# Attention and feed-forward fused: from 128-token tiles with tokens on partitions to 512-token chunks with features on partitions

## The chip, the cores and the metric

The program runs on one core of one Trainium2 chip. A core has a matrix engine (PE; its weight loads are listed as PEld), a vector engine (DVE), an activation engine (ACT), a general engine (POOL) and a queue engine (SP), and 16 DMA engines. Each engine works through its own list of instructions in order; semaphores make one wait for another. SBUF is the on-chip memory, 128 partitions wide; PSUM is the small memory that PE writes, 8 banks of 2 KB a partition. The metric is device time in microseconds (us) of one execution, lower is better.

## The reference

Inputs are `q`, `k`, `v` of shape (8, 8, 576, 64): batch B, heads H, sequence S, head width D. There is no softmax over the sequence; each head has a 64x64 matrix `kv`. Everything is float32 outside the kernel.

```python
kv  = einsum('bhsd,bhse->bhde', k, v)
out = einsum('bhsd,bhde->bhse', q, kv)
x   = out / sqrt(mean(out*out, -1) + 1e-6) * g_norm     # per head; then tokens x (H*D = 512)
h   = x @ w_in                                          # 4608 x 1024
sm  = exp(h - max(h)) / (sum(exp(h - max(h))) + 1e-9)
solu = h * sm
ln  = (solu - mean(solu)) / sqrt(var(solu) + 1e-6) * g_ln
return ln @ w_out                                       # 4608 x 512
```

A layer norm takes out any factor that is common to a row, so both kernels leave the division by the softmax sum undone: they normalise `h * exp(h)` instead. The old kernel puts 1e-30 in place of the 1e-6 under the roots.

## The kernel before, in words

Tokens stand on partitions. The batch is taken in four pairs. For each of the two batches of a pair, `phase_A` loads `k` and `v` in tiles of 128 tokens (the fifth tile has 64), multiplies them per head into `kv_ps` and copies each to `kv_sb`; `phase_B` loads a tile of `q`, transposes it head by head on PE (`qtps`, copied to `qtsb`), multiplies by `kv_sb` into `op`, squares on ACT (`osq`), sums per head on DVE (`ssq`), takes Ln and Exp on ACT (`lssq`, `rstd`) for the reciprocal root, scales (`xb`) and transposes back (`xtps`) into `xT`. Then `phase_C` runs for each 128-token tile: 8 matmuls into `hps` (2 PSUM banks), Exp on ACT (`e_sb`), product on DVE (`solu`), statistics on DVE (`stats`, `mv`), Ln and Exp on ACT (`lvar`, `rstd_ln`), normalisation on DVE (`ln`), 8 transposes (`lnTps`), a copy (`lnT`), 8 matmuls (`ops`), a copy on ACT (`obuf`), and the store from SP's queue.

A scheduler orders each engine's instructions by its own estimates, and so mixes the phases of neighbouring tiles. `hps` has one buffer, `lnTps` and `ops` share one, `op`, `qtps` and `xtps` have one each. All loads go through POOL's DMA queue and change float32 to bf16 on the way; each row that a load moves is one head of one token: 64 values, 256 bytes in DRAM. Weights are loaded first, then scaled by `g_norm` and `g_ln` on DVE.

ACT_TABLE_LOAD is an instruction that the compiler puts into ACT's list where the next function is not in the table that is loaded: here between Ln and Exp.

Of the kernel before, what the change touches and what calls it, by code (L numbers as in the profile page):

```python
# [21 lines left out]
):  # L23
    nc = tc.nc
    fp32 = mybir.dt.float32
    bf16 = mybir.dt.bfloat16
# [25 lines left out]
    kv_sb = big.tile([128, B * H, D], bf16)

    g_rep = big.tile([128, 1], fp32)
    nc.gpsimd.dma_start(g_rep[:64, :], g_norm[:, None])
    nc.gpsimd.dma_start(g_rep[64:128, :], g_norm[:, None])
    g_ln_sb = big.tile([128, 8], fp32)
    for nt in range(8):  # L60
        nc.gpsimd.dma_start(g_ln_sb[:, nt:nt + 1], moe_g_ln[nt * 128:(nt + 1) * 128, None])

    with tc.tile_pool(name="wtmp", bufs=2) as wtmp_pool:
        for dt in range(4):
            wt = wtmp_pool.tile([128, d_ff], bf16, name="wt")
            nc.gpsimd.dma_start(wt[:, :], moe_w_in[dt * 128:(dt + 1) * 128, :])
            nc.vector.tensor_scalar_mul(out=w_in_sb[:, dt, :], in0=wt[:, :], scalar1=g_rep[:, :])
        for ntl in range(8):
            wt = wtmp_pool.tile([128, d_model], bf16, name="wt2")
            nc.gpsimd.dma_start(wt[:, :], moe_w_out[ntl * 128:(ntl + 1) * 128, :])  # L70
            nc.vector.tensor_scalar_mul(out=w_out_sb[:, ntl, :], in0=wt[:, :], scalar1=g_ln_sb[:, ntl:ntl + 1])

    kvl = ctx.enter_context(tc.tile_pool(name="kvl", bufs=12))
    kvp = ctx.enter_context(tc.tile_pool(name="kvp", bufs=2, space=bass.MemoryType.PSUM))
    qload = ctx.enter_context(tc.tile_pool(name="qload", bufs=2))
    qt_p = ctx.enter_context(tc.tile_pool(name="qtp", bufs=1, space=bass.MemoryType.PSUM))
    ap_p = ctx.enter_context(tc.tile_pool(name="attp", bufs=1, space=bass.MemoryType.PSUM))
    xtp = ctx.enter_context(tc.tile_pool(name="xtp", bufs=1, space=bass.MemoryType.PSUM))
    qt_s = ctx.enter_context(tc.tile_pool(name="qts", bufs=2))
    rmsp = ctx.enter_context(tc.tile_pool(name="rmsp", bufs=2))  # L80
    moep = ctx.enter_context(tc.tile_pool(name="moep", bufs=1, space=bass.MemoryType.PSUM))
    Cpsum = ctx.enter_context(tc.tile_pool(name="Cpsum", bufs=1, space=bass.MemoryType.PSUM))
    mpool = ctx.enter_context(tc.tile_pool(name="mpool", bufs=2))
    smallp = ctx.enter_context(tc.tile_pool(name="smallp", bufs=3))

    def phase_A(b):
        kstiles = []
        vstiles = []
        for s0, sz in S_TILES:
            ks = kvl.tile([128, H, D], bf16, name="ks")  # L90
            vs = kvl.tile([128, H, D], bf16, name="vs")
            nc.gpsimd.dma_start(ks[:sz, :, :], k[b, :, s0:s0 + sz, :].rearrange("h s d -> s h d"))  # L92
            nc.gpsimd.dma_start(vs[:sz, :, :], v[b, :, s0:s0 + sz, :].rearrange("h s d -> s h d"))
            kstiles.append(ks)
            vstiles.append(vs)
        nst = len(S_TILES)
        for h in range(H):
            kv_ps = kvp.tile([128, D], fp32, name="kv_ps")
            for sti, (s0, sz) in enumerate(S_TILES):
                nc.tensor.matmul(  # L100
                    kv_ps[:D, :], kstiles[sti][:sz, h, :], vstiles[sti][:sz, h, :],
                    start=(sti == 0), stop=(sti == nst - 1),
                )
            nc.scalar.copy(out=kv_sb[:D, b * H + h, :], in_=kv_ps[:D, :])  # L104

    def phase_B(b):
        for s0, sz in S_TILES:
            qtl = qload.tile([128, H, D], bf16, name="qtl")
            nc.gpsimd.dma_start(qtl[:sz, :, :], q[b, :, s0:s0 + sz, :].rearrange("h s d -> s h d"))  # L109
            qtps = qt_p.tile([128, H, 128], bf16, name="qtps")  # L110
            for h in range(H):
                nc.tensor.transpose(qtps[:D, h, :sz], qtl[:sz, h, :], ident[:sz, :sz])  # L112
            qts = qt_s.tile([128, H, 128], bf16, name="qtsb")
            nc.vector.tensor_copy(qts[:D, :, :sz], qtps[:D, :, :sz])  # L114
            op = ap_p.tile([128, H * D], fp32, name="op")
            for h in range(H):
                nc.tensor.matmul(  # L117
                    op[:sz, h * D:(h + 1) * D], qts[:D, h, :sz], kv_sb[:D, b * H + h, :],
                    start=True, stop=True,
                )  # L120
            opr = op.rearrange("p (h d) -> p h d", h=H)
            osq = rmsp.tile([128, H * D], fp32, name="osq")
            nc.scalar.activation(out=osq[:sz, :], in_=op[:sz, :], func=AF.Square)  # L123
            ssq = rmsp.tile([128, H], fp32, name="ssq")
            nc.vector.tensor_reduce(out=ssq[:sz, :], in_=osq.rearrange("p (h d) -> p h d", h=H)[:sz, :, :], axis=AX, op=ADD)
            lssq = rmsp.tile([128, H], fp32, name="lssq")
            nc.scalar.activation(out=lssq[:sz, :], in_=ssq[:sz, :], func=AF.Ln, scale=1.0 / D, bias=eps_t[:sz, :])  # L127
            rstd = rmsp.tile([128, H], fp32, name="rstd")
            nc.scalar.activation(out=rstd[:sz, :], in_=lssq[:sz, :], func=AF.Exp, scale=-0.5, bias=0.0)  # L129
            xb = rmsp.tile([128, H * D], bf16, name="xb")  # L130
            nc.vector.tensor_tensor(  # L131
                out=xb.rearrange("p (h d) -> p h d", h=H)[:sz, :, :],
                in0=opr[:sz, :, :],
                in1=rstd[:sz, :, None].to_broadcast([sz, H, D]),
                op=MUL,
            )
            xbr = xb.rearrange("p (dt c) -> p dt c", dt=4)
            xtps = xtp.tile([128, 4, 128], bf16, name="xtps")
            for dt in range(4):
                nc.tensor.transpose(xtps[:, dt, :sz], xbr[:sz, dt, :], ident[:sz, :sz])  # L140
            tk0 = b * S + s0
            nc.scalar.copy(out=xT[:, :, tk0:tk0 + sz], in_=xtps[:, :, :sz])  # L142

    def phase_C(m):
        t0 = m * 128
        hps = moep.tile([128, d_ff], fp32, name="hps", tag="hps")
        for dt in range(4):
            for nh in range(2):
                nc.tensor.matmul(  # L149
                    hps[:, nh * 512:(nh + 1) * 512],  # L150
                    xT[:, dt, t0:t0 + 128],
                    w_in_sb[:, dt, nh * 512:(nh + 1) * 512],
                    start=(dt == 0), stop=(dt == 3),
                )
        e_sb = mpool.tile([128, d_ff], fp32, name="e_sb")
        nc.scalar.activation(out=e_sb[:, :], in_=hps[:, :], func=AF.Exp)  # L156
        solu = mpool.tile([128, d_ff], fp32, name="solu")
        nc.vector.tensor_tensor(out=solu[:, :], in0=hps[:, :], in1=e_sb[:, :], op=MUL)  # L158
        stats = smallp.tile([128, 2, 6], fp32, name="stats")
        for sg in range(2):  # L160
            nc.vector.bn_stats(out=stats[:, sg, :], in_=solu[:, sg * 512:(sg + 1) * 512])  # L161
        mv = smallp.tile([128, 2], fp32, name="mv")
        nc.vector.bn_aggr(out=mv[:, :], in_=stats[:, :, :])
        lvar = smallp.tile([128, 1], fp32, name="lvar")
# [7 lines left out]
        for ntl in range(8):  # L172
            nc.tensor.transpose(lnTps[:, ntl, :], lnr[:, ntl, :], ident[:, :])  # L173
# [3 lines left out]
        for ntl in range(8):  # L177
            nc.tensor.matmul(ops[:, :], lnT[:, ntl, :], w_out_sb[:, ntl, :], start=(ntl == 0), stop=(ntl == 7))  # L178
# [44 lines left out]
```

## Time and profile before

| | |
|---|---|
| median of 3 runs | 426.84 us (426.75 to 428.88) |
| span of the profiled execution | 427.0 us |
| PE busy | 282.0 us, 66% |
| ACT busy | 301.2 us, 71% |
| DVE busy | 219.5 us, 51% |
| POOL busy | 114.1 us, 27% |
| mean granted clock of PE | 0.844 |

No total of its own is listed for the profiled execution beside its span. The span lies 0.2 us above the median and inside the range of the runs, so what lies around it is taken as nothing, and sums are made against 427.0 us. Busy shares are means over the whole span. A group's "mean ns" is the duration of one instruction; matmuls overlap, so a group of n can be busy for less than n times the mean.

### The profile page before, as it was taken

The numbers are of one execution on the slowest core, as the hardware profiler recorded it, in microseconds if no ns is written. First come the engines' busy times: TensorE is split into PE (matmuls) and PEld (weight loads), VectorE is DVE, ScalarE is ACT, GpSimd is POOL, SyncE is SP. The second block draws the span as 40 slices with busy tenths as digits, with TensorE's granted clock in tenths as the row PEclk, the third lists the DMA queues.
The fourth block names the chain that finished last, engine by engine and source line by source line (L and its number), as shares of the span: only waits on it lengthen the run. The fifth ranks groups of instructions, "written<-read, shape, count | busy, mean of one in ns | idle before, by whom it ended". The sixth has DMA issues, their size and how long they took to land.

```text
span 427.0 us, 5212 instructions
## 1 busy us (share of the span) xinstructions
PE 282.0 (66%) x1984; PEld 147.8 (35%) x1984; DVE 219.5 (51%) x349; ACT 301.2 (71%) x495; POOL 114.1 (27%) x148
## 2 busy tenths in 40 slices
PE   0112775966977874978786828477876966756755
PEld 0112442543533342544343414233332433332222
DVE  0310324654767473556675736447674655456461
ACT  1000567699786777899868787979769689797771
POOL 8459546546280013650000110100010110000000
PEclk9999976688799896868999988667998668569888
DMA  2989979999695254995232441420340331001011
GB/s 37 148 80 138 109 50 92 77 109 124 61 128 77 38 74 28 108 80 54 40 58 57 50 51 13 42 38 11 52 68 25 65 24 32 25 0 51 25 49 49
DMA packets 119768, 26.03 MB, mean 61 GB/s; under 512 B 113600, under 2 KB 114624, under 8 KB 119744
## 3 DMA queue, kind: packets, MB, share of 16 engines
q0 software_dynamic: 114560, 16.27, 55.4%
q1 hardware_dynamic: 5184, 9.44, 6.0%
q8 instruction: 15, 0.25, 0.2%
q14 instruction: 9, 0.07, 0.1%
HBM read 32.51 MB, written 9.44 MB: 98 GB/s over the span
## 4 chain that ended last, share of the span: by engine, by line
ACT 50%; PE 27%; issue 7%; DVE 7%; DMA 5%; POOL 4%; POOLq 0%
ACT L127 9%; PE hps L149 9%; ACT L165 8%; ACT L129 7%; PE ops L178 6%; ACT e_sb L156 6%; ACT L167 5%; PE lnTps L173 3%; PE kv_ps L100 3%; PE xtps L140 3%; DVE ln L169 3%; ACT obuf L180 2%; DVE xb L131 2%; ACT lssq L127 2%; ACT osq L123 2%
## 5 line engine op out<-in xcount | busy, mean ns | idle before, releaser
L149 PE MATMUL hps<-w_in_sb,xT 128*128 128x512 bf16 x288 | 94.6, 446 | 5.7 <-DVE solu L158 5.6
L109 POOL DMA_DIRECT2D qtl<-in_q_dram x40 | 33.7, 842 | 212.7 <-PE qtps L112 159.1
L178 PE MATMUL ops<-w_out_sb,lnT 128*128 128x512 bf16 x288 | 85.0, 441 | 3.5 <-DVE lnT L175 3.4
L131 DVE TENSOR_TENSOR xb<-op,rstd 128x512 bf16<-128x512 f32 (+1 forms) x40 | 27.4, 685 | 77.7 <-ACT rstd L129 77.7
L156 ACT ACTIVATE e_sb<-hps 128x1024 f32<-128x1024 f32 x36 | 36.7, 1020 | 29.4 <-PE hps L149 29.3
L100 PE MATMUL kv_ps<-vs,ks 128*64 128x64 bf16 (+1 forms) x320 | 33.8, 222 | 33.9 <-ACT kv_sb L104 17.8
L169 DVE TENSOR_SCALAR ln<-solu,mv,rstd_ln 128x1024 bf16<-128x1024 f32 x36 | 29.7, 824 | 49.3 <-ACT rstd_ln L167 49.3
L173 PE MATMUL lnTps<-ident,ln 128*128 128x128 bf16 x288 | 27.6, 252 | 39.8 <-DVE ln L169 31.7
L158 DVE TENSOR_TENSOR solu<-hps,e_sb 128x1024 f32<-128x1024 f32 x36 | 43.6, 1212 | 17.4 <-ACT e_sb L156 17.4
L127 ACT ACT_TABLE_LOAD x37 | 47.5, 1283 | 0.7
L161 DVE BATCH_NORM_STATS2 stats<-solu 128x6 f32<-128x512 f32 x72 | 47.0, 676 | 0.0
L104 ACT CAST kv_sb<-kv_ps 64x64 bf16<-64x64 f32 x64 | 11.5, 200 | 49.1 <-PE kv_ps L100 49.1
L112 PE MATMUL qtps<-ident,qtl 128*64 128x128 bf16 (+1 forms) x320 | 31.2, 247 | 21.8 <-DMA qtl<-in_q_dram 19.9
L178 PEld LDWEIGHTS <-lnT 128*128 128x128 bf16 x288 | 28.3, 109 | 42.4 <-issue 16.3
L129 ACT ACT_TABLE_LOAD x33 | 42.3, 1283 | 0.6
L100 PEld LDWEIGHTS <-ks 128*64 128x64 bf16 (+1 forms) x320 | 24.6, 124 | 49.5 <-issue 40.5
L140 PE MATMUL xtps<-ident,xb 128*128 128x128 bf16 (+1 forms) x160 | 17.5, 241 | 36.5 <-DVE xb L131 33.3
L92 POOL DMA_DIRECT2D ks<-in_k_dram x40 | 35.7, 892 | 18.3 <-PE kv_ps L100 14.7
L149 PEld LDWEIGHTS <-xT 128*128 128x128 bf16 x288 | 27.5, 107 | 35.0 <-issue 18.5
L173 PEld LDWEIGHTS <-ln 128*128 128x128 bf16 x288 | 21.5, 114 | 51.3 <-DVE ln L169 47.5
L114 DVE COPY qtsb<-qtps 64x1024 bf16<-64x1024 bf16 (+1 forms) x40 | 24.7, 617 | 27.4 <-PE op L117 25.3
L142 ACT COPY xT<-xtps 128x512 bf16<-128x512 bf16 (+1 forms) x40 | 21.5, 539 | 21.5 <-PE xtps L140 21.2
(32 smaller groups left out, 337.2 us busy)
## 6 DMA issues: line engine op xcount, KB each, us to landing
out_dram<-obuf SPq DMA_DIRECT2D x36, 256.0 KB, 2.0
qtl<-in_q_dram POOLq DMA_DIRECT2D x32, 128.0 KB, 3.4
ks<-in_k_dram POOLq DMA_DIRECT2D x32, 128.0 KB, 4.4
vs<-in_v_dram POOLq DMA_DIRECT2D x32, 128.0 KB, 4.6
wt<-in_moe_w_in_dram POOLq DMA_DIRECT2D x4, 256.0 KB, 5.1
wt<-in_moe_w_out_dram POOLq DMA_DIRECT2D x8, 128.0 KB, 4.1
qtl<-in_q_dram POOLq DMA_DIRECT2D x8, 64.0 KB, 2.6
ks<-in_k_dram POOLq DMA_DIRECT2D x8, 64.0 KB, 4.3
```

The lines of the kernel that those rows point to most:

```text
L92: nc.gpsimd.dma_start(ks[:sz, :, :], k[b, :, s0:s0 + sz, :].rearrange("h s d -> s h d"))
L100: nc.tensor.matmul(kv_ps[:D, :], kstiles[sti][:sz, h, :], vstiles[sti][:sz, h, :], start=(sti == 0), stop=(sti == nst - 1),)
L127: nc.scalar.activation(out=lssq[:sz, :], in_=ssq[:sz, :], func=AF.Ln, scale=1.0 / D, bias=eps_t[:sz, :])
L129: nc.scalar.activation(out=rstd[:sz, :], in_=lssq[:sz, :], func=AF.Exp, scale=-0.5, bias=0.0)
L131: nc.vector.tensor_tensor(out=xb.rearrange("p (h d) -> p h d", h=H)[:sz, :, :], in0=opr[:sz, :, :], in1=rstd[:sz, :, None].to_broadcast([s ...
L149: nc.tensor.matmul(hps[:, nh * 512:(nh + 1) * 512], xT[:, dt, t0:t0 + 128], w_in_sb[:, dt, nh * 512:(nh + 1) * 512], start=(dt == 0), stop ...
L156: nc.scalar.activation(out=e_sb[:, :], in_=hps[:, :], func=AF.Exp)
L158: nc.vector.tensor_tensor(out=solu[:, :], in0=hps[:, :], in1=e_sb[:, :], op=MUL)
L161: nc.vector.bn_stats(out=stats[:, sg, :], in_=solu[:, sg * 512:(sg + 1) * 512])
L169: nc.vector.tensor_scalar(out=ln[:, :], in0=solu[:, :], scalar1=mv[:, 0:1], scalar2=rstd[:, :], op0=SUB, op1=MUL)
L173: nc.tensor.transpose(lnTps[:, ntl, :], lnr[:, ntl, :], ident[:, :])
L178: nc.tensor.matmul(ops[:, :], lnT[:, ntl, :], w_out_sb[:, ntl, :], start=(ntl == 0), stop=(ntl == 7))
```

## The change

The whole body is rewritten, and the order of work on each engine is now the order in which it is written (`manual_schedule`).

- **Layout.** A chunk has 512 tokens. Chunks 0 to 7 are the first 512 tokens of the 8 batches; chunk 8 is the 64 left-over tokens of all 8. Features stand on partitions and tokens on the free axis, for `q` (transposed on PE into `qT_ps`), `x_sb` and `h_ps`. `u_sb` (the product `h * exp(h)`) is then the stationary operand of the last matmul as it is, so `xtps`, `lnTps` and their copies are gone.
- **Loads.** `load_main` brings 512 tokens of a batch in one DMA, four neighbouring tokens of a head to a row: 1,024 bytes in DRAM. `load_rem` brings the 64 left-over tokens. Loads of a batch are issued three chunks ahead. The weights come in float32 over SP's queue.
- **Attention.** `kvbd` holds two heads' matrices on a block diagonal, so one 128x512 matmul makes `o_ps` for two heads. The sum of squares over a head is a matmul with `head_mean` (`s_ps`); Ln, Exp (`lss`, `rst`) and the scaling then work on 128x512 tiles, 4 for each chunk.
- **Statistics.** POOL squares `u` (`usq_sb`) and adds pairs of `e` (`es_sb`). Twenty matmuls with 32-column weights (`stat_sel`, four groups of columns in turn) sum squares, `u` and `e` over the features into `sum_ps`; DVE copies it to `sums`; four float32 matmuls bring it to tokens on partitions (`st_ps`); DVE and ACT make `rstd` from it.
- **Layer norm folded.** `w_out_sb` is `g_ln * w_out` less its mean over the features (`mean_ps`), which takes out the mean of `u`; `rstd` is applied when the result leaves PSUM (`out_evac`, on DVE).
- **Tables.** One table that has Exp, Ln and Square is loaded at the start.
- **Pipeline.** Chunk c has 8 slots. In slot s PE makes `h_ps` of c, a part of the attention of c+1 (in slot 6 the `kv` of c+2), and half of one output tile of c-1.

```diff
+    ctx.enter_context(tc.manual_schedule())
+    epool = ctx.enter_context(tc.tile_pool(name="epool", bufs=4))
+    ph = ctx.enter_context(tc.tile_pool(name="ph", bufs=2, space=PSUM))
+    po = ctx.enter_context(tc.tile_pool(name="po", bufs=2, space=PSUM))
+    pst = ctx.enter_context(tc.tile_pool(name="pst", bufs=1, space=PSUM))
+    pat = ctx.enter_context(tc.tile_pool(name="pat", bufs=3, space=PSUM))
+    nc.scalar.preload_act_table_set("natural_log_exp_and_others")
...
+    def s_mm(c, p):
+        t = pat.tile([128, 512], FP32, name="s_ps", tag="at")
+        nc.tensor.matmul(t[:, :], head_mean[:, :], osq_sb.pop(p)[:, :], start=True, stop=True)
+        lss = work.tile([128, 512], FP32, name="lss")
+        nc.scalar.activation(out=lss[:, :], in_=t[:, :], func=AF.Ln, bias=eps_t[:, :])
+        rst = work.tile([128, 512], FP32, name="rst")
+        nc.scalar.activation(out=rst[:, :], in_=lss[:, :], func=AF.Exp, scale=-0.5, bias=zero_t[:, :])
+        nc.vector.tensor_tensor(out=x_sb[c][:, p, :], in0=o_ps.pop(p)[:, :], in1=rst[:, :], op=MUL)
...
+    def h_step(c, f):
...
+        t = ph.tile([128, 512], FP32, name="h_ps")
+        for dt in range(NP):
+            nc.tensor.matmul(
+                t[:, :], w_in_sb[:, dt, f * 128:(f + 1) * 128], x_sb[c][:, dt, :],
+                start=(dt == 0), stop=(dt == NP - 1),
+            )
...
+        nc.scalar.activation(out=e[:, f % 2, :], in_=t[:, :], func=AF.Exp, bias=zero_t[:, :])
+        nc.vector.tensor_tensor(out=u_sb[c][:, f, :], in0=t[:, :], in1=e[:, f % 2, :], op=MUL)
+        nc.gpsimd.tensor_tensor(out=usq_sb[c][:, f, :], in0=u_sb[c][:, f, :], in1=u_sb[c][:, f, :], op=MUL)
+        if f % 2 == 1:
+            nc.gpsimd.tensor_tensor(out=es_sb[c][:, f // 2, :], in0=e[:, 0, :], in1=e[:, 1, :], op=ADD)
...
+    def stats(c):
+        t = pst.tile([128, 512], FP32, name="sum_ps", tag="st")
...
+        for n, (i, mov) in enumerate(todo):
+            j = n % 4
+            nc.tensor.matmul(
+                t[32 * j:32 * j + 32, :], stat_sel[:, i, :], mov,
+                start=(n < 4), stop=(n >= len(todo) - 4), tile_position=(0, 32 * j),
+            )
+        sums = work.tile([128, 512], FP32, name="sums")
+        nc.vector.tensor_copy(sums[:, :], t[:, :])
+        st_ps = pst.tile([128, 4, 3], FP32, name="st_ps", tag="st")
+        for m in range(4):
+            nc.tensor.matmul(st_ps[:, m, :], sums[:, m * 128:(m + 1) * 128], stat_pick[:, :], start=True, stop=True)
...
+    for c in range(NC + 1):
+        for s in range(8):
+            if c < NC:
+                h_step(c, s)
+            if c >= 1 and s == 0:
+                stats(c - 1)
+            if c == 0:
+                if s < 4:
+                    for f in (2 * s, 2 * s + 1):
+                        nc.gpsimd.tensor_scalar_mul(
+                            out=w_out_g[:, f, :], in0=w_out_f[:, f, :], scalar1=g_ln_sb[:, f:f + 1]
+                        )
+                if s == 5:
...
+                        nc.tensor.matmul(mean_ps[:, :], col_mean[:, :], w_out_g[:, f, :], start=(f == 0), stop=(f == NF - 1))
...
+            if c + 1 < NC:
+                a = c + 1
...
+                if s == 0:
+                    qT(a, 0)
+                if s == 1:
+                    qT(a, 1)
+                    o_mm(a, 0)
+                if 2 <= s <= 5:
+                    s_mm(a, s - 2)
+                    if s < 5:
+                        o_mm(a, s - 1)
+                if s == 6 and c + 2 < B:
+                    kv_mm(c + 2)
+                    kv_evac(c + 2)
+            if s == 2 and c + 3 < B:
+                load_main(ks, kvl, k, c + 3, "ks")
...
+            if c >= 1:
+                out_half(c - 1, s // 2, s % 2)
+                if s % 2 == 1:
+                    out_evac(c - 1, s // 2)
```

**ACT, in the middle of the program.** Before, from one Ln of the attention (`lssq`) to the next:

```order
L127 ACT_TABLE_LOAD
L127 ACTIVATE lssq<-ssq,eps_t 128x8
L129 ACT_TABLE_LOAD
L129 ACTIVATE rstd<-lssq 128x8
L165 ACT_TABLE_LOAD
L165 ACTIVATE lvar<-mv,eps_t 128x1
L167 ACT_TABLE_LOAD
L167 ACTIVATE rstd_ln<-lvar 128x1
L156 ACTIVATE e_sb<-hps 128x1024
L142 COPY xT<-xtps 128x4x128
L123 ACTIVATE osq<-op 128x512
```

The same engine now, in slots 1 to 3 of a chunk (line numbers are those of the changed kernel):

```order
L206 ACTIVATE osq<-o_ps,zero_t 128x512
L234 ACTIVATE e_sb<-h_ps,zero_t 128x512
L212 ACTIVATE lss<-s_ps,eps_t 128x512
L214 ACTIVATE rst<-lss,zero_t 128x512
L206 ACTIVATE osq<-o_ps,zero_t 128x512
L234 ACTIVATE e_sb<-h_ps,zero_t 128x512
```

The table loads are out of the list, the copies `xT` and `obuf` too, and Ln and Exp of the attention work on 512 columns instead of 8.

**POOL, in the middle of the program before.** Its list holds nothing but DMA issues there:

```order
L92 DMA ks<-in_k_dram 128x8x64
L93 DMA vs<-in_v_dram 128x8x64
L92 DMA ks<-in_k_dram 64x8x64
L93 DMA vs<-in_v_dram 64x8x64
L92 DMA ks<-in_k_dram 128x8x64
```

POOL now, in slots 0 to 3 of chunk 0 (`w_out_g` is scaled there once; in later chunks those rows are absent):

```order
L236 TENSOR_TENSOR usq_sb<-u_sb 128x512
L320 TENSOR_SCALAR w_out_g<-w_out_f,g_ln_sb 128x512 x2
L236 TENSOR_TENSOR usq_sb<-u_sb 128x512
L238 TENSOR_TENSOR es_sb<-e_sb 128x512
L320 TENSOR_SCALAR w_out_g<-w_out_f,g_ln_sb 128x512 x2
L236 TENSOR_TENSOR usq_sb<-u_sb 128x512
L320 TENSOR_SCALAR w_out_g<-w_out_f,g_ln_sb 128x512 x2
L74 DMA ks<-in_k_dram 128x8x256
L74 DMA vs<-in_v_dram 128x8x256
L236 TENSOR_TENSOR usq_sb<-u_sb 128x512
```

POOL now computes between its DMA issues, 12 products and sums a chunk, and a DMA issue stands behind the computations ahead of it.

**DVE, in the middle of the program before**, where statistics of one tile stand among the copies of others:

```order
L163 BN_AGGR mv<-stats 128x2
L161 BN_STATS stats<-solu 128x6
L169 TENSOR_SCALAR ln<-solu,mv,rstd_ln 128x1024
L114 COPY qtsb<-qtps 64x1024
L125 TENSOR_REDUCE ssq<-osq 128x8
L175 COPY lnT<-lnTps 128x1024
L131 TENSOR_TENSOR xb<-op,rstd 128x512
```

DVE now, in slots 0 and 1 of a chunk, where PE's `st_ps` matmuls wait for `sums` and its outputs for `rstd`:

```order
L235 TENSOR_TENSOR u_sb<-h_ps,e_sb 128x512
L254 COPY sums<-sum_ps 128x512
L259 COPY st<-st_ps 128x12
L261 TENSOR_TENSOR sq<-st 128x8
L263 TENSOR_TENSOR var<-st,sq 128x4
L265 SCALAR_TENSOR_TENSOR vare<-sq,var 128x4
L189 COPY qT_sb<-qT_ps 128x1024
```

BN_STATS, BN_AGGR and the normalisation `ln` are gone from DVE; statistics come once a chunk, as a chain between PE and DVE.

More of the change, by code (lines that the diff above doesn't have):

```diff
@@ L54 @@
[L54 to L99, printed above, removed]
+    assert (B, H, S, D) == (8, 8, 576, 64) and d_model == H * D and n_tok == B * S
@@ L100, in phase_A @@
                 nc.tensor.matmul(
-                    kv_ps[:D, :], kstiles[sti][:sz, h, :], vstiles[sti][:sz, h, :],
-                    start=(sti == 0), stop=(sti == nst - 1),
-                )
[L104 to L135, printed above, removed]
-            )
[L137 to L164, printed above, removed]
-        nc.scalar.activation(out=lvar[:, :], in_=mv[:, 1:2], func=AF.Ln, bias=eps_t[:, :])
-        rstd = smallp.tile([128, 1], fp32, name="rstd_ln")
-        nc.scalar.activation(out=rstd[:, :], in_=lvar[:, :], func=AF.Exp, scale=-0.5, bias=0.0)
-        ln = mpool.tile([128, d_ff], bf16, name="ln")
-        nc.vector.tensor_scalar(out=ln[:, :], in0=solu[:, :], scalar1=mv[:, 0:1], scalar2=rstd[:, :], op0=SUB, op1=MUL)
-        lnTps = Cpsum.tile([128, 8, 128], bf16, name="lnTps", tag="C")
-        lnr = ln.rearrange("p (nt c) -> p nt c", nt=8)
-        for ntl in range(8):
-            nc.tensor.transpose(lnTps[:, ntl, :], lnr[:, ntl, :], ident[:, :])
-        lnT = mpool.tile([128, 8, 128], bf16, name="lnT")
-        nc.vector.tensor_copy(lnT[:, :, :], lnTps[:, :, :])
-        ops = Cpsum.tile([128, d_model], fp32, name="ops", tag="C")
-        for ntl in range(8):
-            nc.tensor.matmul(ops[:, :], lnT[:, ntl, :], w_out_sb[:, ntl, :], start=(ntl == 0), stop=(ntl == 7))
-        obuf = mpool.tile([128, d_model], fp32, name="obuf")
-        nc.scalar.copy(out=obuf[:, :], in_=ops[:, :])
-        nc.sync.dma_start(out[t0:t0 + 128, :], obuf[:, :])
```

242 lines of the change are left out of this document (216 added, 26 removed).

## The prediction

> **What bounds the kernel now.** I read the page's busy shares and its chain first, then the groups with shapes kept apart, then one period of the timeline.
>
> ```profile
> span 427.0 us, 5212 instructions
> PE 282.0 (66%) x1984; PEld 147.8 (35%) x1984; DVE 219.5 (51%) x349; ACT 301.2 (71%) x495; POOL 114.1 (27%) x148
> ...
> ACT 50%; PE 27%; issue 7%; DVE 7%; DMA 5%; POOL 4%; POOLq 0%
> ```
>
> No engine is full. ACT is the busiest and holds half of the chain that ended last. What it is busy with:
>
> ```profile
> L127 ACT ACT_TABLE_LOAD x37 | 47.5, 1283 | 0.7
> L129 ACT ACT_TABLE_LOAD x33 | 42.3, 1283 | 0.6
> L156 ACT ACTIVATE e_sb<-hps 128x1024 f32<-128x1024 f32 x36 | 36.7, 1020 | 29.4 <-PE hps L149 29.3
> L167 ACT ACT_TABLE_LOAD x28 | 35.9, 1283 | 0.5
> L165 ACT ACT_TABLE_LOAD x26 | 33.4, 1283 | 0.5
> L123 ACT ACTIVATE osq<-op 128x512 f32<-128x512 f32 x32 | 19.2, 600 | 1.4 <-PE op L117 1.4
> L127 ACT ACTIVATE lssq<-ssq,eps_t 128x8 f32<-128x8 f32 x32 | 9.6, 299 | 3.6 <-DVE ssq L125 3.3
> L129 ACT ACTIVATE rstd<-lssq 128x8 f32<-128x8 f32 x32 | 6.6, 206 | 0.3
> ```
>
> The four rows of table loads sum to 159.1 us, over half of ACT's time. One period of the feed-forward shows them on the path:
>
> ```profile
> 311.98 1.02 ACT L156 ACTIVATE e_sb<-hps 128x1024 f32<-128x1024 f32 x1 [1.67 <-PE hps L149]
> ...
> 313.02 1.28 ACT L165 ACT_TABLE_LOAD   x1
> ...
> 314.82 1.28 ACT L167 ACT_TABLE_LOAD   x1
> ...
> 316.35 0.81 DVE L169 TENSOR_SCALAR ln<-solu,mv,rstd_ln 128x1024 bf16<-128x1024 f32 x1 [1.99 <-ACT rstd_ln L167]
> ...
> 318.74 1.02 ACT L156 ACTIVATE e_sb<-hps 128x1024 f32<-128x1024 f32 x1 [1.86 <-PE hps L149]
> ```
>
> A tile takes 6.76 us, as a ring: Exp, load, Ln, load, Exp, normalise, transposes, `hps`. ACT, DVE and PE take turns. The bound is this ring and ACT together.
>
> **What goes.** All but one of the table loads (the new ACT list has one), the transposes of `xb` and `ln` with their copies, and the ring itself: statistics come once for 512 tokens and only the store needs them. ACT then has 20 activations of 512 columns a chunk. One without a bias tile took 0.60 (`osq`); a bias tile costs 0.09 more (299 against 206 ns on 8 columns); so 20 x 0.69 + 0.5 = 14.3 us a chunk. DVE: 12 products at the `xb` row's 0.69, five passes over a PSUM bank at about the same, two copies at 0.68, two of `kv` at up to 0.69, four small ones at 0.2: 15.3 us.
>
> ```profile
> L131 DVE TENSOR_TENSOR xb<-op,rstd 128x512 bf16<-128x512 f32 x32 | 22.0, 686 | 63.7 <-ACT rstd L129 63.7
> L175 DVE COPY lnT<-lnTps 128x1024 bf16<-128x1024 bf16 x36 | 24.5, 681 | 4.3 <-PE lnTps L173 3.8
> L109 POOL DMA_DIRECT2D qtl<-in_q_dram x40 | 33.7, 842 | 212.7 <-PE qtps L112 159.1 <-PE kv_ps L100 48.6 <-DMA qtl<-in_q_dram 4.8
> masks.py:199 POOL TENSOR_SCALAR_AFFINE_SELECT ident<-ident 128x128 bf16<-128x128 bf16 x1 | 0.3, 304 | 0.1
> ```
>
> POOL's products have no row. Below: DVE's 0.69. Above: the one 128-column pass took 0.304, four times that is 1.2 for 512 columns, and twice again for a second input is 2.4. I take 1.2, the nearest row scaled: 12 x 1.2 plus about 4.5 us of DMA issues (three at 0.84 and three shorter) is 19 us. The Trainium skill, "GPSIMD Engine Reference", section 3.1, gives 4,497 ns for a two-input add of 2,048 float32 columns, an estimate of 1.12 us for 512; by it POOL would need 18 us and the sum below would not move; no run here shows it yet.
>
> **PE, the new bound.** Prices from the timeline and two groups:
>
> ```profile
> 57.59 0.81 PE L100 MATMUL kv_ps<-vs,ks 128*64 128x64 bf16 x10 [0.86 <-ACT kv_sb L104]
> ...
> 301.37 0.38 PE L149 MATMUL hps<-w_in_sb,xT 128*128 128x512 bf16 x1
> ...
> 305.30 1.90 PE L178 MATMUL ops<-w_out_sb,lnT 128*128 128x512 bf16 x8
> ...
> 313.99 0.63 PE L112 MATMUL qtps<-ident,qtl 128*64 128x128 bf16 x8
> ...
> 415.27 3.59 PE L178 MATMUL ops<-w_out_sb,lnT 128*128 128x512 bf16 x8 [0.79 <-DVE lnT L175]
> ```
>
> ```profile
> L149 PE MATMUL hps<-w_in_sb,xT 128*128 128x512 bf16 x288 | 94.6, 446 | 5.7 <-DVE solu L158 5.6
> L173 PEld LDWEIGHTS <-ln 128*128 128x128 bf16 x288 | 21.5, 114 | 51.3 <-DVE ln L169 47.5 <-issue 3.2
> ```
>
> At full clock a 512-column matmul in a row of them costs (1.90 - 0.38) / 7 = 0.217 us, weight load hidden; at half clock 3.59 / 8 = 0.45. Small ones of `kv` and the transposes cost about 0.06 each once the tail of the last is taken off. A steady chunk:
>
> - `h_ps` 32 x 0.217 = 6.9; output 32 x 0.217 = 6.9; `o_ps` and `s_ps` 8 x 0.217 = 1.7.
> - `qT_ps` 32 x 0.06 = 1.9; `kv` 40 x 0.06 = 2.4. Both alternate between two halves of the columns; if these run side by side the two fall by half, 2.1 less.
> - `sum_ps`: 20 matmuls, no row with 32 columns. Side by side in four groups 5 x 0.217 = 1.1, one after another 4.3. But the last needs `usq_sb` and `es_sb` of the slot just before: from the end of the last `h_ps`, Exp 0.69, product 0.69, two POOL passes 2.4, 3.9 with the hand-overs, while PE has 1.7 of other work. So at least 2.5; I take 3.0.
> - `sums`: PE waits while DVE copies, 0.16 + 0.69 + hand-overs = 1.0. Queued behind: the transposes and the output of slot 0, that wait with it.
> - `st_ps`: 4 float32 matmuls with three columns. Below, four weight loads of 0.114, 0.5; above, four times the 0.446 mean of a full matmul, 1.8. I take 1.2.
> - Waits on ACT: in slots 2 to 5 ACT has four activations, 2.6 us, against PE's 10 x 0.217 = 2.2; `s_ps` needs the last of the four. 3 x 0.43 = 1.3. In slot 6 `kv` needs the bank of `o_ps`, held until the last `x_sb`: 0.5.
>
> Sum 26.8 us. ACT, DVE and POOL are under it, so their work is covered; with a cover gone the next bound would be POOL.
>
> The Trainium skill, "TensorEngine Tiling", Key Properties, says that a change of tiling mode drains the engine, which speaks against mixing 128-, 64- and 32-column matmuls. Priced as a lone matmul's 0.38 against 0.217 in a row, some nine changes a chunk would be 1.5 us and the total about 12 us more. No row here shows it.
>
> **Start, chunk 0, end.** Loads:
>
> ```profile
> q0 software_dynamic: 114560, 16.27, 55.4%
> q1 hardware_dynamic: 5184, 9.44, 6.0%
> ...
> 99.35:102.76 3.41, 3.41 (x27) 0.98 2.23 142
> ```
>
> A packet of q0 took 0.554 x 427 x 16 / 114,560 = 33 ns (128 bytes written), one of q1 79 ns (2,048 bytes). New rows of 512 bytes: 50 ns, between them. Before the first `q` has landed, 3 x 1,024 of these, 2,048 small ones and, on the other queue, 2,048 of the weights': 384 us over 16 engines, 24 us, plus 2 to the first issue. The window's share of 2.23 shows two packets of an engine at once, so as little as 14. I take 26, since both queues compete. After that: 32 transposes at half clock 3.8, copy 0.7, `o_ps` and square 1.1, four rounds of Ln, Exp and product partly overlapped, 8.5. The first `h_ps` starts at 40 (28 to 44). In steady chunks 3 x 1,024 x 50 ns / 16 = 10 us of loads hide under 26.8.
>
> Chunk 0: POOL has 6 products, 8 scalings of `w_out_g` and 2 issues ahead of `mean_ps`: 14 x 1.2 + 1.8 = 18.6, from 2.2 after the start; then 1.7 of `mean_ps` and 4.2 of slots 6 and 7: 27 (22 to 32).
>
> Chunks 1 to 5: 134. Chunks 6 and 7 lack `kv`: 2 x 23.9 = 48. Chunk 8 lacks the attention: 19. End: statistics 3.5 + 1.0 + 1.2, output 6.9, its copy 0.7, store and finish 3.2 as now (the row below ends at 423.8 of 427.0): 16.5.
>
> ```profile
> 423.23 0.58 ACT L180 COPY obuf<-ops 128x512 f32<-128x512 f32 x1 [3.75 <-PE ops L178]
> ```
>
> 40 + 27 + 134 + 48 + 19 + 16.5 = **284 us** against a span of 427.0, 0.2 above the median. With all low ends (22 a steady chunk) 28 + 22 + 110 + 39 + 17 + 15 = 231; with all high ones (31) 44 + 32 + 155 + 56 + 22 + 18 = 327.
>
> **Rivals.**
>
> 1. POOL becomes the bound. At 2.4 us a pass, 12 x 2.4 + 4.5 = 33 us a chunk and 52 in chunk 0: 40 + 52 + 5 x 33 + 3 x 29 + 14 = 358. It decides from 1.9 us a pass. For it: POOL has hardly computed so far. Against it: the one scaled row.
>
> 2. PE falls to half clock in part of each chunk. Five windows of 3.41 us show how this goes now:
>
> ```profile
> 160.79:164.20 3.41, 0.00 (x0) 1.00 0.60 38
> 164.20:167.62 3.42, 1.02 (x10) 0.52 0.00 0
> 167.62:171.03 3.41, 3.41 (x26) 0.50 0.72 46
> 171.03:174.44 3.41, 3.41 (x22) 0.50 2.11 134
> 174.44:177.86 3.42, 3.42 (x34) 0.98 0.58 37
> ```
>
> A window without PE work is followed by three at half, two of them fully busy. Slot 0 with its waits is the quietest stretch now; one drop of 6.8 us a chunk would lose 3.4 each, 284 + 9 x 3.4 = 315. The Trainium skill, "TensorE: Matmul & The Clock Gate", Part 1, has one busy window of about 3.4 us bring the full clock back; here it took more, and by the page the loss would be half, 299. Against the rival: PE would be over 80% busy, and waits of 1 us are far below 3.4.
>
> 3. Slower: the gate keeps PE at half clock throughout. Every PE term doubles, about 24 a steady chunk: 284 + 24 x 5 + 21 x 2 + 18 + 24 = 488. It passes 427 once 70% of PE's work runs at half. Now the mean granted clock is 0.844 with PE 66% busy; more work in a row speaks against it.
>
> 4. Everything small runs side by side and nothing waits: 231 to 248, say 242.
>
> **Chances.** Forecast 0.61, its own range 252 to 312. Rival 1: 0.13, rival 2: 0.13, rival 4: 0.11, rival 3: 0.02. Range 250 to 320: it takes in rival 2, half of rival 1's lower part and cuts off 358 and the lowest sums. About 0.5% can be told from no change; no case ends within it but by chance: faster 0.97, same 0.01, slower 0.02.
>
> **What would show it.** ACT with one table load and under 180 us busy; the distance between two `sums` copies 26 to 28 us in chunks 2 to 5; the PE wait before `st_ps` near 1 us, eight to nine times; POOL's product at 1.2 us; `h_ps` first at 40 us; granted clock over 0.9. The prediction is wrong if POOL's rows stand at 2 us or if PE waits for POOL for more than 2 us a chunk, if the clock stays near 0.84, or if the first `q` lands after 35 us.

## The result, and the profile after

The changed kernel takes **290.4 us** (four runs, 288.2 to 292.7) against 426.8 us (426.2 to 428.9): a ratio of 0.679 with an interval of 0.674 to 0.683. Forecast were 284 us and a range of 250 to 320. The profiled execution took 292.7 us, the slowest of the four (granted clock 0.912; the others 0.911 to 0.928); its span is 290.9 us, and the sums below are made against that span.

The page of the changed kernel begins with span and busy shares; further down stand the granted clock in 40 slices, the queue of the loads (packets, MB, share of 16 engines), and the chain that ended last.

```profile
span 290.9 us, 3927 instructions
PE 220.5 (76%) x1528; PEld 102.2 (35%) x1528; DVE 140.0 (48%) x251; ACT 123.1 (42%) x199; POOL 171.8 (59%) x171
...
PEclk9999999959599859997996699799999979979979
...
q0 software_dynamic: 37632, 14.16, 42.1%
...
PE 37%; POOL 24%; ACT 13%; DMA 10%; DVE 7%; issue 6%; POOLq 0%; ACTq 0%; DVEq 0%
```

ACT has gone from 301.2 to 123.1 us and from 50% of the chain to 13%. PE is the busiest engine now. POOL, with DMA issues alone and 4% of the chain before, holds a quarter of it. The clock row dips again and again, each time for one or two slices of 7.3 us.

The groups of the changed kernel, shapes kept apart, that answer to terms of the forecast (the last fields are the idle time of the engine just before them, and what ended it):

```profile
L60 ACT ACT_TABLE_LOAD x1 | 1.3, 1283 | 0.7 <-PEq L379 0.7
...
L236 POOL TENSOR_TENSOR usq_sb<-u_sb 128x512 bf16<-128x512 bf16 x72 | 75.0, 1043 | 87.4 <-DVE u_sb L235 87.3
L238 POOL TENSOR_TENSOR es_sb<-e_sb 128x512 bf16<-128x512 f32 x36 | 45.9, 1275 | 0.0
...
L257 PE MATMUL st_ps<-stat_pick,sums 128*128 128x3 f32 x72 | 12.2, 292 | 7.2 <-DVE sums L254 7.2
L249 PE MATMUL sum_ps<-usq_sb,stat_sel 128*32 128x512 bf16 x72 | 10.4, 384 | 8.8 <-POOL usq_sb L236 8.8
...
L320 POOL TENSOR_SCALAR w_out_g<-w_out_f,g_ln_sb 128x512 bf16<-128x512 f32 x8 | 12.4, 1559 | 0.0
```

One table load is left of 127. A square on POOL takes 1.04 us, a sum of two tiles of `e` 1.28. The scaling of `w_out` takes 1.56 us, though it reads one tile and a column. PE waited 7.2 us for `sums` and 8.8 for the squares.

Next, the changed kernel from one `sums` copy to the next, for chunks 2 to 6; the edges are the starts of the copies. The columns are the length, then busy time and instructions of PE, PEld, DVE, ACT and POOL, the granted clock, the DMA share and GB/s.

```profile
101.48:128.77 27.29, 24.74 (x172) 11.84 (x172) 14.23 (x25) 13.46 (x22) 16.96 (x18) 0.84 0.64 102
128.77:156.04 27.27, 23.75 (x172) 10.74 (x172) 14.13 (x25) 13.46 (x22) 20.02 (x22) 0.91 0.80 111
156.04:183.35 27.31, 24.77 (x172) 11.85 (x172) 14.22 (x25) 13.47 (x22) 15.65 (x16) 0.84 0.57 97
183.35:208.66 25.31, 22.77 (x172) 10.53 (x172) 14.13 (x25) 13.46 (x22) 13.19 (x13) 0.93 0.12 43
208.66:231.37 22.71, 20.17 (x132) 9.24 (x132) 13.28 (x23) 13.46 (x22) 13.19 (x13) 1.00 0.13 47
```

A chunk takes the 27 us of the forecast where the clock is 0.84 to 0.91; chunk 5, at 0.93, takes 25.3. The last row, at 1.00 and without `kv`, takes 22.7. Where the clock goes is seen at the boundary between two chunks, in PE's timeline of the changed kernel (start, length, work; in brackets the wait before it):

```profile
127.12 0.38 PE L249 MATMUL sum_ps<-usq_sb,stat_sel 128*32 128x512 bf16 x1 [0.35 <-POOL usq_sb L236]
127.13 0.80 PE L249 MATMUL sum_ps<-u_sb,stat_sel 128*32 128x512 bf16 x8
...
128.36 0.38 PE L249 MATMUL sum_ps<-es_sb,stat_sel 128*32 128x512 bf16 x1 [0.41 <-POOL es_sb L238]
129.52 1.05 PE L257 MATMUL st_ps<-stat_pick,sums 128*128 128x3 f32 x8 [0.79 <-DVE sums L254]
...
131.51 1.89 PE L280 MATMUL out_ps<-w_out_sb,u_sb 128*128 128x512 bf16 x4
...
135.33 1.03 PE L280 MATMUL out_ps<-w_out_sb,u_sb 128*128 128x512 bf16 x4
```

Three waits of 0.35, 0.41 and 0.79 us, and then four output matmuls take 1.89 us instead of 1.03. Two places of the changed kernel in windows, cut where the clock changes:

```profile
96.36:99.78 3.42, 1.70 (x14) 0.42 (x16) 1.70 (x3) 0.69 (x1) 3.42 (x5) 1.00 1.49 225
99.78:103.19 3.41, 2.63 (x18) 1.30 (x10) 0.69 (x1) 0.00 (x0) 2.03 (x2) 0.51 0.53 99
103.19:106.60 3.41, 3.41 (x25) 2.23 (x25) 1.36 (x5) 0.59 (x2) 0.00 (x0) 0.50 0.02 5
106.60:110.00 3.40, 3.40 (x23) 1.46 (x22) 0.62 (x2) 0.69 (x1) 0.00 (x0) 0.50 0.00 0
...
127.12:130.53 3.41, 2.21 (x23) 1.32 (x22) 1.31 (x2) 0.00 (x0) 2.19 (x2) 1.00 0.40 127
130.53:133.94 3.41, 3.41 (x23) 1.69 (x23) 1.35 (x5) 0.59 (x2) 0.00 (x0) 0.50 0.00 0
133.94:137.35 3.41, 3.41 (x30) 1.65 (x29) 1.95 (x3) 1.41 (x3) 1.22 (x2) 1.00 0.00 0
```

A window in which PE was 50% or 65% busy is followed by half clock, for three windows in one place and for one in the other. The Trainium skill, "TensorE: Matmul & The Clock Gate", Part 1, lets the clock fall after at least one idle window of about 3.4 us and return after at least one busy one. In the second place one fully busy window was enough for the return; in the first the clock was still low in the window after a fully busy one (103.19), and neither window ahead of a drop was idle.

### The profile page after: what moved, and what is told of

It is laid out like the page before. It is cut to its first block, busy times and chain, and to the rows that moved or that the text cites. A ratio compares the mean times of both kernels' runs of the same rounds, so it can differ in the third digit from the quotient of the medians.

```text
span 290.9 us, 3927 instructions
## 1 busy us (share of the span) xinstructions
PE 220.5 (76%) x1528; PEld 102.2 (35%) x1528; DVE 140.0 (48%) x251; ACT 123.1 (42%) x199; POOL 171.8 (59%) x171
## 3 DMA queue, kind: packets, MB, share of 16 engines
q0 software_dynamic: 37632, 14.16, 42.1%
## 4 chain that ended last, share of the span: by engine, by line
PE 37%; POOL 24%; ACT 13%; DMA 10%; DVE 7%; issue 6%; POOLq 0%; ACTq 0%; DVEq 0%
PE out_ps L280 14%; PE h_ps L227 10%; POOL usq_sb L236 9%; DMA vs<-in_v_dram 6%; POOL es_sb L238 6%; ACT e_sb L234 5%; PE st_ps L257 4%; DMA ks<-in_k_dram 4%; POOL w_out_g L320 4%; ACT rst L214 3%; PE qT_ps L184 3%; DVE u_sb L235 3%; ACT lss L212 3%; ACT osq L206 3%; DVE sums L254 2%
## 5 line engine op out<-in xcount | busy, mean ns | idle before, releaser
L236 POOL TENSOR_TENSOR usq_sb<-u_sb 128x512 bf16<-128x512 bf16 x72 | 75.0, 1043 | 87.4 <-DVE u_sb L235 87.3
L227 PE MATMUL h_ps<-x_sb,w_in_sb 128*128 128x512 bf16 x288 | 80.7, 405 | 0.8 <-DVE x_sb L215 0.8
L280 PE MATMUL out_ps<-w_out_sb,u_sb 128*128 128x512 bf16 x288 | 80.7, 411 | 0.0
L235 DVE TENSOR_TENSOR u_sb<-h_ps,e_sb 128x512 bf16<-128x512 f32 x72 | 49.6, 688 | 55.4 <-ACT e_sb L234 55.3
L234 ACT ACTIVATE e_sb<-h_ps,zero_t 128x512 f32<-128x512 f32 x72 | 49.3, 685 | 61.9 <-PE h_ps L227 61.9
L238 POOL TENSOR_TENSOR es_sb<-e_sb 128x512 bf16<-128x512 f32 x36 | 45.9, 1275 | 0.0
L227 PEld LDWEIGHTS <-w_in_sb 128*128 128x128 bf16 x288 | 29.8, 104 | 40.8 <-issue 12.0
L280 PEld LDWEIGHTS <-u_sb 128*128 128x128 bf16 x288 | 28.5, 104 | 37.2 <-issue 11.7
L288 DVE TENSOR_SCALAR ob<-out_ps,rstd 128x512 f32<-128x512 f32 x36 | 26.7, 743 | 6.4 <-PE out_ps L280 6.4
L214 ACT ACTIVATE rst<-lss,zero_t 128x512 f32<-128x512 f32 x36 | 26.0, 722 | 1.2
L152 PE MATMUL kv_ps<-vs,ks 128*64 128x64 bf16 x256 | 6.7, 214 | 15.7 <-DMA vs<-in_v_dram 15.7
```

What stands on the lines that cost most here:

```text
L214: nc.scalar.activation(out=rst[:, :], in_=lss[:, :], func=AF.Exp, scale=-0.5, bias=zero_t[:, :])
L227: nc.tensor.matmul(t[:, :], w_in_sb[:, dt, f * 128:(f + 1) * 128], x_sb[c][:, dt, :], start=(dt == 0), stop=(dt == NP - 1),)
L234: nc.scalar.activation(out=e[:, f % 2, :], in_=t[:, :], func=AF.Exp, bias=zero_t[:, :])
L235: nc.vector.tensor_tensor(out=u_sb[c][:, f, :], in0=t[:, :], in1=e[:, f % 2, :], op=MUL)
L236: nc.gpsimd.tensor_tensor(out=usq_sb[c][:, f, :], in0=u_sb[c][:, f, :], in1=u_sb[c][:, f, :], op=MUL)
L238: nc.gpsimd.tensor_tensor(out=es_sb[c][:, f // 2, :], in0=e[:, 0, :], in1=e[:, 1, :], op=ADD)
```

## The experiments

Two theories were to be told apart first. One says that the gain is the table loads; the other that it is the new layout and its loads. Three runs split that.

**The old kernel with one table.** One line is added to the old kernel; its table loads go from 127 to 1. The scheduler also mixes the phases in another order on every engine, so what follows holds for both together.

```diff
+    nc.scalar.preload_act_table_set("natural_log_exp_and_others")
```

> The kernel before with one line added, the load of one table that has Exp, Ln and Square; 126 of its 127 table loads are then gone from ACT's list, and the scheduler mixes the phases a little differently. Theory A (the table loads sat in the ring of every tile and were the largest single cost): the ring of 6.76 us loses two loads, so 36 tiles save some 70 us and the attention stages 20 to 40 more; 310 to 350 us. Rival B (the loads mostly stood beside other work, and the new layout brought the gain): over 395 us.

Measured: 296.6 us (294.6 to 299.4), ratio to the old kernel 0.693 (0.690 to 0.697). That is below what either theory gave. Its page and two windows of 100 us from its middle show why:

```profile
PE 236.5 (80%) x1984; PEld 132.6 (45%) x1984; DVE 217.7 (74%) x349; ACT 138.1 (47%) x369; POOL 115.0 (39%) x148
...
PE 57%; DVE 14%; DMA 10%; POOL 8%; ACT 6%; issue 4%; POOLq 0%
```

```profile
40.00:140.00 100.00, 94.43 (x854) 56.00 (x854) 78.25 (x122) 54.61 (x162) 66.64 (x78) 0.98 1.57 122
140.00:240.00 100.00, 96.20 (x790) 52.24 (x790) 89.61 (x143) 55.91 (x145) 18.43 (x22) 0.97 0.53 71
```

With the loads gone from the ring, PE is 94 to 96% busy at a clock of 0.97 to 0.98. It is busy for 236.5 us now; it was 282.0 with the same 1,984 matmuls, because the granted clock was 0.844. The 126 loads that are gone had 161.7 us of ACT's time (126 x 1.283), and the kernel is 130 us shorter, 1.03 us for each: a part of them stood beside other work. But a part of their price was paid on PE, whose busy time fell by 45.5 us as the clock rose. One line, with the order that the scheduler then makes, brings 130 of the 136 us that the whole rewrite brings. On the table loads the Trainium skill, "ScalarE: Activation LUTs", "Table sets: the hidden batching unit", names this set as holding both Exp and Ln, so that the two together need one load; the trace agrees (127 loads before, 1 now).

**The new kernel without the table.** The same line is taken out of the new kernel; 91 loads stand in ACT's list instead of one.

```diff
-    nc.scalar.preload_act_table_set("natural_log_exp_and_others")
```

> The changed kernel without its table preload: 91 table loads come back, two for each of the four Ln and Exp pairs of a chunk and two for its statistics. Theory A (slots 2 to 5 are a ring over ACT): each of these slots goes from 2.6 to 5.2 us on ACT, PE has 2.2, so 4 x 2.6 = 10 us a chunk for 8 chunks, 10 at the start, 2 to 3 at each boundary: 380 to 410 us. Rival B (ACT was busy for 123 of 291 us, so 115 us more fit into its idle time): 288 to 305 us.

Measured: 370.2 us (369.5 to 370.7), ratio 0.867 (0.865 to 0.870). The loads cost 80 us in the new kernel, 0.89 for each of the 90 added, somewhat less than the first theory gave; the second falls. Here the order on the engines is fixed, so this difference is the loads alone. One of its rows of loads on ACT (another 55 are in others), and PE's longest sum of waits (total, times, longest):

```profile
L211 ACT ACT_TABLE_LOAD x36 | 46.2, 1283 | 0.6
```

```profile
PE s_ps L209 <- ACT osq L205: 51.2, 24, 3.8
```

The rest of the rewrite is thus worth 426.8 - 370.2 = 57 us with the loads present and 296.6 - 290.4 = 6 us without them. The two gains are not additive, since the old kernel without loads keeps PE busy nearly throughout already.

**Narrow loads in the new kernel.** Each wide load becomes four with rows of 256 bytes in DRAM.

```diff
-        nc.gpsimd.dma_start(
-            t.rearrange("p h j d -> p h (j d)"),
-            src[b, :, 0:512, :].rearrange("h (p j) d -> p h (j d)", j=4),
-        )
+        for j in range(4):
+            nc.gpsimd.dma_start(
+                t[:, :, j, :],
+                src[b, :, 0:512, :].rearrange("h (p j) d -> j p h d", j=4)[j],
+            )
```

> The changed kernel with each wide load split into four DMAs with rows of 256 bytes, as in the kernel before; the data in SBUF are the same. Theory A (row width counts through POOL and through the start): POOL has 9 more issues a chunk at 0.9 us, 8 us, which brings it to about 26 us against PE's 27, and the first q lands some 12 us later: 305 to 335 us. Rival B (loads are hidden, only the start moves): 292 to 303 us.

Measured: 340.6 us (339.9 to 342.4), ratio 0.798 (0.795 to 0.802). Dearer than expected. Its busy shares, its waits, its first queue, and the chain:

```profile
PE 232.2 (68%) x1528; PEld 106.0 (31%) x1528; DVE 141.1 (42%) x251; ACT 123.2 (36%) x199; POOL 234.5 (69%) x243
...
q0 software_dynamic: 112512, 14.16, 66.4%
...
POOL 48%; PE 29%; ACT 7%; DMA 7%; DVE 4%; issue 3%; POOLq 0%; ACTq 0%
```

```profile
PE sum_ps L250 <- POOL usq_sb L237: 32.3, 22, 5.2
```

POOL is busy 62.7 us longer with the 72 issues added, and the squares stand behind them in its list. PE waits 32.3 us for squares instead of 8.8 and 18.0 for `mean_ps` instead of 7.1, while its wait for the first loads grew only from 15.7 to 23.4. By these waits the wide loads matter here more as work taken off POOL, which this layout needs for its statistics, than as packets on the queue; no run changes the packets alone. The old kernel with one table has narrow rows too, but its POOL computes nothing (39% busy), and its PE is 94 to 96% busy all the same.

The next four runs ask what the drops of the clock cost and which wait makes them.

**Filler in PE's waits.** Eight output matmuls whose result is overwritten are added at each boundary: four ahead of the last two squares of the statistics, and four that run while DVE copies `sums`. The tile that they write is the one that the output then begins anew.

```diff
+        def filler():
+            for f in range(4):
+                nc.tensor.matmul(fill[:, :], u_sb[c][:, f, 0:128], w_out_sb[:, f, :], start=True, stop=True)
...
+            if n == 6:
+                filler()
...
+        filler()
```

> The changed kernel with PE given eight extra output matmuls at each chunk boundary, four where it waits for POOL's last squares and four where it waits for the copy of the sums; their results are overwritten. The waits were 0.4 to 1.7 and 0.8 us, the added work is 0.87 each at full clock, so by itself it would cost 0 to 1 us a chunk. Theory A (PE's clock drops at the boundaries because these waits leave a quiet window): the granted clock rises from 0.91 to over 0.96 and the time falls by 5 to 20 us, to 270 to 285. Rival B (the drops come from the 32-column and float32 matmuls or from the position of the windows): the clock stays at 0.90 to 0.93 and the time is 288 to 300.

Measured: 276.4 us (274.7 to 277.6), ratio 0.647 (0.644 to 0.651). Seventy-two matmuls more, and 14 us less. Its clock row, and its chunks 2, 3 and 4 from copy to copy:

```profile
PEclk9999957975999999999999999999999999999999
```

```profile
99.04:122.74 23.70, 22.69 (x181) 10.54 (x181) 14.05 (x26) 13.47 (x22) 17.18 (x18) 1.00 0.73 116
122.74:148.18 25.44, 23.27 (x181) 10.72 (x180) 14.05 (x25) 13.47 (x22) 19.81 (x22) 1.00 0.84 119
148.18:171.88 23.70, 22.69 (x181) 10.56 (x181) 14.05 (x25) 13.48 (x22) 15.87 (x16) 1.00 0.66 113
```

The clock stays whole after chunk 0, and the chunks that took 27.3 us take 23.7 to 25.4. That PE's idleness at the boundary takes the clock is shown: the run keeps POOL's passes, the copy of `sums`, and the 32-column and float32 matmuls, and only fills the time beside them. What the drops cost is at least these 14 us, since the added matmuls are still in the time.

**The turn later.** `stats` is split behind the copy of `sums`; the `st_ps` matmuls stand behind the first half of the output of tile 0.

```diff
             if c >= 1 and s == 0:
                 stats(c - 1)
+                out_half(c - 1, 0, 0)
+                stats_turn(c - 1)
...
-                out_half(c - 1, s // 2, s % 2)
+                if s > 0:
+                    out_half(c - 1, s // 2, s % 2)
```

> The changed kernel with the four st_ps matmuls and what follows them placed behind the first half of output tile 0, so that PE has 0.87 us of work while DVE copies sums; the wait for POOL's last squares stays. Theory A (each PE wait at the boundary costs its length, and the two together cost the clock): 9 x 0.8 = 7 us from the wait, and with less quiet time at the boundary fewer drops, 3 to 8 us more: 274 to 282. Rival B (only the waits count, the clock stays at 0.91 to 0.93): 281 to 285. Rival C (the chain behind st_ps to rstd becomes late for the first output copy, which holds DVE): 285 to 292.

Measured: 271.7 us (267.9 to 272.9), ratio 0.632 (0.628 to 0.636), a little better than the first theory gave. In the profiled execution the clock drops in chunk 0 (59.7 us), at the first two boundaries (73.3 and 100.7) and at the end, and no more between:

```profile
PEclk9999999995959995999999999999999999999997
```

```profile
PE sum_ps L250 <- POOL usq_sb L236: 8.7, 12, 2.5
```

The wait for POOL's squares is as long as before; the wait for `sums` is off the list, since output matmuls now stand in its place.

**The statistics a slot later.** `stats` moves from slot 0 to slot 1, so POOL has a slot more; the copy of output tile 0 moves to slot 2.

```diff
-            if c >= 1 and s == 0:
+            if c >= 1 and s == 1:
                 stats(c - 1)
...
+                if s == 2:
+                    out_evac(c - 1, 0)
-                if s % 2 == 1:
+                if s % 2 == 1 and s > 1:
```

> The changed kernel with the statistics matmuls moved from slot 0 to slot 1 of the next chunk (behind its second h_ps), and the copy of output tile 0 from slot 1 to slot 2. PE's wait for POOL (11.6 us in all) goes, the wait for sums (7.2) stays. Theory A: 290 - 11 and fewer drops of the clock: 270 to 280. Rival B (PE was to wait there anyhow, for ACT in slots 2 to 5, since the attention comes later by as much): 284 to 291.

Measured: 271.5 us (268.5 to 272.3), ratio 0.635 (0.631 to 0.639). The wait for squares is gone, and the chunks are down to 23 to 24 us. But the clock still drops, at most boundaries:

```profile
PEclk9999957975979997999999799799979999999868
```

```profile
PE st_ps L257 <- DVE sums L254: 9.2, 9, 2.3
```

Here the wait for `sums` stays. Taken with the run before: with that wait gone the drops stop in the middle of the program though the POOL wait stays, and with the POOL wait gone they go on, at six of the nine boundaries. One execution of each is profiled, and the mean clocks of the four executions overlap (0.956 to 0.976 with the later turn, 0.915 to 0.962 here), so this is a sign and no proof that the wait for `sums` is the worse of the two; the times are the same.

What share of a window has to be busy isn't settled. In each of these traces the changes of the clock lie on a grid of 3.41 us (in the changed kernel the drops at 72.5, 99.8, 130.5 and 154.4 us are 8, 9 and 7 windows apart). Cut on that grid, a window of this run with PE busy 2.49 of 3.41 us is followed by half clock, and in the run before a window with 1.92 of 3.41 kept the full clock:

```profile
145.78:149.19 3.41, 2.49 (x28) 1.75 (x28) 1.75 (x5) 0.00 (x0) 3.31 (x4) 1.00 0.54 99
149.19:152.60 3.41, 3.41 (x10) 1.21 (x8) 0.89 (x3) 1.53 (x4) 0.00 (x0) 0.50 0.00 0
```

```profile
148.44:151.85 3.41, 1.92 (x16) 0.63 (x16) 0.63 (x2) 0.00 (x0) 3.41 (x4) 1.00 1.34 215
151.85:155.27 3.42, 3.42 (x47) 2.30 (x45) 1.66 (x6) 0.93 (x3) 0.24 (x1) 1.00 0.03 4
```

(The first fence is this run, the second the one with the later turn.) So PE's busy share of one window does not decide by itself; what does stays open.

**The scaling of `w_out` on DVE.** This is for chunk 0 alone.

```diff
-                        nc.gpsimd.tensor_scalar_mul(
+                        nc.vector.tensor_scalar_mul(
```

> The changed kernel with the eight scalings of w_out_g on DVE instead of POOL (12.4 us of POOL in chunk 0, where PE waits 7.1 us for mean_ps). DVE needs about 0.4 us each, half of the 0.77 that it takes for 1,024 columns. Theory A (POOL's queue sets chunk 0): 280 to 284. Rival B (the loads that queue behind, or the squares, are late next, so the wait moves to the statistics of chunk 0): 286 to 291.

Measured: 280.5 us (278.6 to 285.9), ratio 0.657 (0.655 to 0.660), as the first theory had it. The scaling costs DVE 0.89 us each instead of POOL's 1.56, but 0.4 was expected. POOL's first three squares, which run beside it, take 1.20 to 1.21 us instead of 1.04; why both are longer there was not tested. The first copy of `sums` comes at 66.4 us instead of 73.5:

```profile
L320 DVE TENSOR_SCALAR w_out_g<-w_out_f,g_ln_sb 128x512 bf16<-128x512 f32 x8 | 6.8, 885 | 0.0
```

```profile
L254 DVE COPY sums<-sum_ps x9: 684/692/692, 66.4 to 263.3; 128x512 f32<-128x512 f32 x9
```

**All three together.** Statistics in slot 1, the turn behind the output half that stands there, and the scaling on DVE.

```diff
-            if c >= 1 and s == 0:
+            if c >= 1 and s == 1:
                 stats(c - 1)
+                out_half(c - 1, 0, 1)
+                stats_turn(c - 1)
...
-                        nc.gpsimd.tensor_scalar_mul(
+                        nc.vector.tensor_scalar_mul(
```

> The three edits together: statistics in slot 1, output work between the sums and st_ps, w_out_g on DVE. Theory A (PE then has work at every boundary, so the clock holds as with the added matmuls, without their 0.87 x 18 = 16 us): 276 - 16 x 0.7 - 7 = 250 to 262, granted clock over 0.96, a chunk in 23 to 24.5 us. Rival B (ACT in slots 2 to 5 and the kv bank set the chunk at 25 or more): 264 to 275.

Measured: 251.3 us (250.4 to 252.2), ratio 0.590 (0.588 to 0.592). This beats both kernels, and the old kernel with one table by 296.6 - 251.3 = 45 us: that is what the rewrite is worth beside the table once its order is mended. Its page, and a chunk from copy to copy:

```profile
span 249.9 us, 3921 instructions
PE 198.0 (79%) x1528; PEld 92.8 (37%) x1528; DVE 146.3 (59%) x259; ACT 121.9 (49%) x199; POOL 160.4 (64%) x163
...
PEclk9999999999979999999999999999999999999997
```

```profile
91.51:113.82 22.31, 20.80 (x174) 9.86 (x174) 14.45 (x25) 13.25 (x22) 17.65 (x18) 1.00 0.82 135
```

The same 1,528 matmuls keep PE busy for 198.0 us instead of 220.5. The longest wait that is left is at the start, where PE waits for the first loads for some 25 us; nothing was tried on that.

## Why the prediction was right, and where two errors met

The forecast of 284 lies 6.4 us under the measured median, and its mechanism held: ACT's table loads and the ring go, PE becomes the bound, and a chunk takes about 27 us. But that figure hides two errors in the steady chunk, which nearly cancel: the small matmuls were priced too high, and there was no term for the clock. That the sum comes out so close is luck.

- **Start, 40.** The first `q` was worked on at 25.9 us (taken: 26), `h_ps` began at 36.7, and its fourth matmul, which had to wait for the last `x_sb`, ran at 39.1. A packet of q0 took 0.421 x 290.9 x 16 / 37,632 = 52 ns, against the 50 taken between two rows.
- **Chunk 0, 27.** Mis-sized. The last `h_ps` ended near 67.8, 31 us after the first. The term had every pass of POOL at 1.2 us; the squares took 1.04 and the sums 1.28, but the eight scalings 1.56, and `mean_ps` waited 7.1 us for them. A one-input pass from float32 was dearer here than a product of two bf16 tiles. The run with the scaling on DVE took this back.
- **Steady chunk, 26.8.** Measured 28.0, three times 27.3, and 25.3: 135 us for five, against 134; the last lies under the 26 to 28 that the prediction named for chunks 2 to 5. `sum_ps` runs side by side (eight in 0.80 us), `kv` as well (32 in 0.69), 16 transposes take 0.64; so `kv` costs 0.9 instead of 2.4 and the transposes 1.3 instead of 1.9. `st_ps` took 1.05 (taken 1.2), the wait for `sums` 0.79 (taken 1.0), and waiting for POOL comes to (8.8 + 2.8) / 9 = 1.3 us a chunk. The filler run, whose chunks take 23.7 to 25.4 at a clock of 1.00, puts the chunk without drops 3 us lower; the drops gave that back.
- **Chunks 6, 7 and 8.** 22.7, 24.0 and 19.8, against 23.9, 23.9 and 19.
- **End, 16.5.** From the last copy of `sums` 15.7 us, where the terms gave 13.0; the output took 8.63 instead of 6.9, with 3.4 us of it at half clock:

```profile
276.99 8.63 PE out_ps L280 x32
```

The differences add up: 3.0 by the first copy (73.5; the terms give 40 + 27 + 3.5), 0.9 over the eight distances, 2.7 at the end. That is 6.6, and 284 becomes 290.6, against a span of 290.9.

**The rivals.** POOL as the bound needed 1.9 us a pass; it is at 1.04 to 1.28. The estimate from the Trainium skill, "GPSIMD Engine Reference", section 3.1, 1.12 us, lies between the two. The drop of the clock, rival 2, is the one that came partly true, inside the forecast's own range: a drop at eight of nine boundaries, five of them of one window, one of two and two of three, where the prediction took two for each. The filler run is 14 us shorter with its added work, and PE's busy time is 22.5 us shorter in the last run with the same matmuls; the rival was priced at 31, and at 15 in the variant by the Trainium skill, "TensorE: Matmul & The Clock Gate", Part 1. The argument against it, that waits of 1 us are far below 3.4, is the step that failed: several short waits in one window can be enough. Half clock throughout did not come: 0.912. The sum with all low ends was right about what runs side by side, and for the rest it needed the mended order: 251.3.

**Which part brings it.** The prediction priced the rewrite as one. It saw that the table loads were over half of ACT's time but never asked what the old kernel would do without them. By its own rows the answer was in reach: PE had 282.0 us of work at a clock of 0.844, some 238 us at full clock. The drain at a change of mode, which the Trainium skill, "TensorEngine Tiling", Key Properties, states and the prediction priced at some 1.5 us a chunk, was not measured by itself. In the last run a chunk has PE busy for 20.8 us. Of these 6.9 + 6.9 + 1.7 + 1.3 + 0.9 + 1.1 + 1.05 = 19.9 are matmuls at the prices above. That leaves about 0.9 for it, as an estimate: what those prices hold of it already is not told apart.

## What to carry to other kernels

Ask of a rewrite first what its cheapest line does alone: an activation engine that swaps tables in a ring can be freed with one line, and the rest of the change is then measured against that kernel. Where PE is the bound, look at the waits between two stages not by their length but by the stretch that they make quiet; work that is there anyway, placed in that gap, can be worth more than the wait (here 19 us for waits of 7, in the run with the later turn). And look at what stands behind a DMA issue in the same engine's list when that engine also computes.

## What the runs showed that was not expected

- Waits of 0.35 to 0.79 us within one window of 3.4 us were followed by a window at half clock, and 72 needless matmuls made the kernel 14 us faster. A window with PE busy 1.92 of 3.41 us kept the clock in one run, and one with 2.49 lost it in another.
- Table loads on ACT cost PE its clock too: without 126 of them, 161.7 us of load time, the kernel is 130 us shorter, and PE's own busy time fell by 45.5 us, from 282.0 to 236.5, as the mean clock rose from 0.844 to 0.980.
- On POOL a pass with a column from float32 to bf16 took 1.56 us for 512 columns, a product of two bf16 tiles 1.04. On DVE the former took 0.89.
- Matmuls with 32-column weights in four column groups ran side by side: eight of 512 columns in 0.80 us, where eight full ones in a row take 1.90.
